# Channel attention and a gated MLP on one core: every engine's order from a planner, second bank seeded by a copy, five gate tiles

## The chip, the core and the metric

The kernel runs on 1 core of one Trainium2 chip. The metric is device time in microseconds: before, 2226.33 us, the median of three runs (2221.29 to 2227.1). TensorE (PE, with its weight loads as PEld), VectorE (DVE), ScalarE (ACT) and GpSimd (POOL) compute; SyncE (SP) issues the DMAs. Each engine works through its own list of instructions in order, and semaphores hold an instruction until its inputs are there.

## The reference

```python
B, N, C = (4, 6080, 256); d_ff = 2048
qn = q / (norm(q, axis=1) + 1e-06)          # q, k, v: (B, N, C) float32
kn = k / (norm(k, axis=1) + 1e-06)
s = kn.transpose(0, 2, 1) @ qn / tau        # C x C for each of 4 batches
a = exp(s - s.max(-1)); a /= a.sum(-1) + 1e-09
x = (v @ a).reshape(B * N, C)               # 24320 tokens
h = x @ w_in                                # w_in, w_out: float64
g = h * (1 / (1 + exp(-1.702 * h)))
out = (g @ w_out).astype(float32)
```

## The kernel before, in words

Every float32 product is made of rounded parts: a high part `h` (a cast by ACT, called `gh`, `vh`, `wh`, `qs`, `ks`) and the rest `l` (a subtraction on DVE, `gl`, `vl`, `wl`), and three matmuls, h by h, h by l, l by h.

Since `(v @ a) @ w_in = v @ (a @ w_in)`, each batch first gets its 256 x 256 matrix `a` from the scores (on PE, in the bank `s`, from q and k in 24 units of 2 x 128 tokens), its norms and a softmax, and then folded weights `a @ w_in`. These are combined with a Strassen scheme of seven products. The tokens of a batch go by in 6 chunks (five of 1024, one of 960), a chunk in two halves `n` of 512 (or 480) columns. For each chunk, 8 *pairs* of 128 hidden rows (`f` = 0, 1) are computed: 4 batches x 6 chunks x 8 pairs = 192 pairs.

A pair is seven products of three matmuls, into the PSUM banks `ps_x`, `ps_y`, `ps_z`. By the names of the new code, with the weight part and the part of `v` of each: m5 (z, 3, 3), m1 (x, 0, 0), m2 (y, 1, 1), m6 (x, 4, 4), m7 (x, 5, 5), m3 (z, 6, 2), m4 (x, 2, 6). The parts of `v` lie in tiles `px`, `py` (two buffers each) and `pz`, `pw` (one buffer), made from two loads, sums on POOL (line 500) and casts. Between the products ACT copies a bank to SBUF (`copied`, line 548: `r5` of z behind m5, `r1` of x behind m1, `r2` of x behind m6), and DVE adds (lines 562, 569, 571: `y + r1`, `x + r5` behind m7, `z + r2` behind m3). Out of these come four blocks, for each a gate (line 585, the activation, then its cast and low part) and a second projection `project` (line 604): six matmuls into one of two pairs of banks `ps_o`, summed over 16 hidden rows, then copied to `osb` (lines 614, 616) and stored.

Work beside it: in the first batch, w_in and w_out come as float64 words and are converted (`to_float32`, lines 131 to 145) during the first eight pairs, and each group of folded weights is made there. During each batch the next one's q and k are loaded, squared (ACT), added (POOL, line 267), split and multiplied, and its softmax and weights follow.

The order: pairs have four slots. `Hidden.slot` issues the products, and one `project` follows each slot, of the pair before in slots 0 to 2, and of block (0, 0) of the same pair in slot 3. Side work hangs on numbered slots. From the first pair on only PE keeps this order (`manual_schedule(engines={PE})`); the orders of DVE, ACT, POOL and SP come from a scheduler when the kernel is built, apart from what is `pinned` behind the newest copy.

Of the kernel before, what the change touches and what calls it, by code (L numbers as in the profile page):

```python
# [18 lines left out]
P = 128  # L19
# [8 lines left out]
def channel_attention_then_glu(  # L28
# [45 lines left out]
    gp = ctx.enter_context(tc.tile_pool(name="gp", bufs=2))  # L74
    op = ctx.enter_context(tc.tile_pool(name="op", bufs=2))
# [42 lines left out]
    def to_float32(out, raw, shape):  # L118

        lw = raw[..., 0]
        hw = raw[..., 1]
        z = cv.tile(shape, U32, tag="z", name="z")
        zf = z.bitcast(F32)
        eighths = cv.tile(shape, U32, tag="low", name="eighths")  # L130
        nc.scalar.activation(zf, hw.bitcast(F32), AF.Abs)
        nc.scalar.activation(eighths, lw, AF.Copy, scale=2.0**-29)
        yield
        nc.vector.tensor_scalar(zf, zf, F64_TOP, F64_BOTTOM, op0=ALU.min, op1=ALU.max)

        nc.vector.tensor_scalar(
            z, z, 5, 2, op0=ALU.logical_shift_left, op1=ALU.logical_shift_right
        )
# [6 lines left out]
        nc.vector.tensor_tensor(out.bitcast(U32), z, eighths, op=ALU.add)  # L145
        return out

    words = {}
# [14 lines left out]
    def win_convert(n):  # L163
        g, c = divmod(n, NC2)
        win[n] = sp.tile([P, GW], F32, tag=("raw_q", "raw_k")[c], name="win")
        yield from to_float32(win[n], words.pop(("in", n)), [P, GW])
# [7 lines left out]
    def wout_convert(u):  # L174
        t = yield from to_float32(None, words.pop(("out", u)), [P, 2, C])
        yield
        fs = slice(2 * u, 2 * u + 2)
        yield from split_parts(wo_h[:, fs, :], wo_l[:, fs, :], t)

    fetch = {"in": win_fetch, "out": wout_fetch}  # L180
    convert = {"in": win_convert, "out": wout_convert}


    class Attention:
        def __init__(self, b, direct=0):
# [5 lines left out]
            self.firsts = {}  # L191
# [54 lines left out]
        def prepare(self, u):  # L246
            nt = self.units[u][1]
            rq, rk = self.fetched(u)
            if u < self.direct:
                qs, ks = rq, rk  # L250
            else:

                qs = sp.tile([P, UT, 2, C], F32R, tag="qs", name="qs")
                ks = sp.tile([P, UT, 2, C], F32R, tag="ks", name="ks")
                for s, r in ((qs, rq), (ks, rk)):
                    split(s[:, :nt, 0, :], s[:, :nt, 1, :], r)
            for r, nm in ((rq, "acc_q"), (rk, "acc_k")):
                if u == 0:
                    acc = small.tile([P, UT, C], F32, tag=nm, name=nm)
                    setattr(self, nm, acc)  # L260
                    nc.scalar.activation(acc, r, AF.Square)
                else:
                    acc = getattr(self, nm)[:, :nt, :]
                    sq = sp.tile([P, UT, C], F32, tag="sq", name="sq", bufs=2)[:, :nt, :]
                    nc.scalar.activation(sq, r, AF.Square)  # L265
                    eng = nc.vector if self.alone else nc.gpsimd
                    eng.tensor_tensor(acc, acc, sq, op=ALU.add)  # L267
            return qs, ks
# [42 lines left out]
        def norms_a(self, meanwhile=None):  # L311

            assert UT == 2
            ps = bank("b", "ps_n")
            for n in range(2 * NC2):
                acc, i = (self.acc_q, self.acc_k)[n // NC2], n % NC2
                if i == 0:
                    eng = nc.vector if self.alone else nc.gpsimd
                    eng.tensor_tensor(acc[:, 0, :], acc[:, 0, :], acc[:, 1, :], op=ALU.add)
                nc.tensor.matmul(  # L320
                    ps[:, n : n + 1],
# [4 lines left out]
            if meanwhile is not None:  # L326
                meanwhile()
            self.rn = small.tile([P, 2 * NC2], F32, tag="rn", name="rn")
            nc.vector.tensor_copy(self.rn, ps[:, : 2 * NC2])
# [11 lines left out]
        def norms_c(self):  # L341

            ps = bank("c" if self.alone else "b", "ps_b")
            for i in range(NC2):
                nc.tensor.matmul(
                    ps[:, i * P : (i + 1) * P], lhsT=ones, rhs=self.diag[:, i, :],
                    start=True, stop=True,
                )
            self.rq = sp.tile([P, C], F32, tag="sq", name="rq", bufs=2)
            nc.vector.tensor_copy(self.rq, ps[:, :C])  # L350

        def softmax_a(self, meanwhile=None):
# [12 lines left out]
            if not self.alone:  # L365

                nc.vector.tensor_scalar_mul(m, m, -1.0)
            if meanwhile is not None:
                meanwhile()
            for i in range(NC2):  # L370
                x, z, mi = self.x[:, i, :], self.z[:, i : i + 1], m[:, i : i + 1]
                nc.scalar.activation(x, x, AF.Exp, bias=mi, accum_out=z)

            nc.scalar.activation(m, m, AF.Gelu_apprx_sigmoid)
# [9 lines left out]
        def transposes(self, meanwhile=None):  # L384
            self.aT_h = small.tile([P, NC2, C], F32R, tag="aT_h", name="aT_h")
            self.aT_l = small.tile([P, NC2, C], F32R, tag="aT_l", name="aT_l")
            ps = bank("b", "ps_t")
            psv = ps.rearrange("p (c x) -> p c x", c=NC2)
            for j in range(NC2):
                for i in range(NC2):  # L390
                    nc.tensor.transpose(  # L391
                        psv[:, j, i * P : (i + 1) * P],
# [3 lines left out]
            if meanwhile is not None:  # L396
                meanwhile()
            split(self.aT_h, self.aT_l, psv)
# [10 lines left out]
        def win_split(self, g, step=split):  # L409
            self.win_h, self.win_l = (  # L410
                sp.tile([P, NC2, GW], F32R, tag=t, name=n)
                for t, n in (("qs", "win_h"), ("ks", "win_l"))
            )
            done = [
                step(self.win_h[:, c, :], self.win_l[:, c, :], win.pop(NC2 * g + c))
                for c in range(NC2)
            ]
            if step is split:
                self.win_keep(g)
            return done  # L420
# [6 lines left out]
        def weights(self, g, i):  # L427
# [7 lines left out]
            ps = bank("ac"[i] if self.alone and g == 0 else "b", "ps_w")  # L435
            ci = slice(i * P, (i + 1) * P)
# [12 lines left out]
            src = ps.rearrange("p (q f n) -> p f q n", q=2, f=2)  # L449
            nc.scalar.copy(self.wf[0][:, (slice(0, 4, 3), slice(1, 3))[i]], src)  # L450

        def weight_sums(self, g):

            t, u = self.wf
            eng = nc.vector if self.alone and g == 0 else nc.gpsimd
            eng.tensor_tensor(u[:, 1], t[:, 0], t[:, 3], op=ALU.subtract)
            eng.tensor_tensor(t[:, 3], t[:, 3], t[:, 2], op=ALU.add)
            eng.tensor_tensor(u[:, 0], t[:, 3], t[:, 0], op=ALU.subtract)
            eng.tensor_tensor(u[:, 2], t[:, 1], u[:, 0], op=ALU.subtract)

        def weight_split(self, g, part, pair=None):

            if part == 0 and not pair:
# [3 lines left out]
            pairs = slice(0, 2) if pair is None else slice(pair, pair + 1)  # L467
            split(
# [408 lines left out]
```

## Time and profile before

| | |
|---|---|
| median of three runs | 2226.33 us |
| the profiled execution | 2224.45 us, span of its instructions 2222.7 us |
| PE, DVE, ACT, POOL busy | 2173.2, 1325.4, 1558.1, 432.0 us |
| granted TensorE clock, mean | 0.996 |
| matmuls recorded | 9952 |

Busy time is the time in which an instruction of the engine is under way. A matmul's end is modelled and lies behind the start of the next, so PE's busy time tells less than the distance between starts. The idle time of PE is given where no matmul is under way, with the engine and line that ended it.

### The profile page before, as it was taken

The page shows a single profiled execution, that of the slowest core. Times are in us where ns is not written, and L with a number is a line of the kernel's source. Part 1 is how long each engine was busy: PE and PEld are TensorE (multiplying, and loading weights), DVE is VectorE, ACT ScalarE, POOL GpSimd, SP SyncE. Part 2 cuts the span into 40 slices and gives each one's busy share as a digit, 9 for nine tenths or more (in the row PEclk, how much of TensorE's full clock was granted, in tenths as well). Part 3 has the DMA queues.
Part 4 walks back from the last instruction along what each step waited for, and adds up shares of the span by engine and source line. Part 5 has one row for each costly group of instructions (what it writes and reads, how often), then busy time and mean ns, then how long its engine had stood idle before and what let it go on. Part 6 is the DMA issues. An engine that isn't in the chain of part 4 may idle for free. (4 is left out here: it accounts for less than half of the span.)

```text
span 2222.7 us, 27468 instructions
## 1 busy us (share of the span) xinstructions
PE 2173.2 (98%) x9952; PEld 1807.5 (81%) x9952; DVE 1325.4 (60%) x1894; ACT 1558.1 (70%) x2769; POOL 432.0 (19%) x348
## 2 busy tenths in 40 slices
PE   8889999999999999999999999999999999999998
PEld 7668787888887888888888888788888888888887
DVE  7986646556555565665655656656555555555454
ACT  6777667767677776776767777677667666666665
POOL 1122313211121232231121213223112110010000
PEclk9999999999999999999999999999999999999999
DMA  9422213112111221221211212122012110111010
GB/s 350 149 85 69 76 48 95 55 66 65 50 64 48 76 86 58 76 60 60 66 57 56 89 47 84 58 76 73 29 56 76 37 57 20 39 57 30 27 37 18
DMA packets 72121, 151.47 MB, mean 68 GB/s; under 512 B 6704, under 2 KB 14128, under 8 KB 71984
## 3 DMA queue, kind: packets, MB, share of 16 engines
q1 hardware_dynamic: 71984, 149.71, 20.4%
q8 instruction: 78, 1.28, 0.2%
q14 instruction: 59, 0.48, 0.1%
HBM read 120.59 MB, written 29.10 MB: 67 GB/s over the span
## 5 line engine op out<-in xcount | busy, mean ns | idle before, releaser
L90 DVE TENSOR_TENSOR gl<-g,gh 128x512 fp32r<-128x512 f32 (+1 forms) x576 | 432.5, 757 | 334.9 <-ACT gh L89 334.7
L604 PE MATMUL ps_o<-gh,wo_l 128*128 128x512 f32 (+1 forms) x1536 | 596.9, 389 | 5.5 <-DVE wo_l L96 5.5
L604 PE MATMUL ps_o<-gh,wo_h 128*128 128x512 f32 (+1 forms) x1536 | 597.0, 389 | 1.5 <-ACT gh L89 1.0
L604 PE MATMUL ps_o<-gl,wo_h 128*128 128x512 f32 (+1 forms) x1536 | 472.6, 389 | 5.7 <-DVE gl L90 5.7
L89 ACT CAST gh<-g 128x512 fp32r<-128x512 f32 (+1 forms) x576 | 351.0, 618 | 9.9 <-PE ps_o L604 1.0
L604 PEld LDWEIGHTS ps_o<-gl,wo_h 128*128 128x128 f32 x1536 | 288.2, 188 | 67.1 <-DVE gl L90 9.8
L604 PEld LDWEIGHTS ps_o<-gh,wo_l 128*128 128x128 f32 x1536 | 289.0, 188 | 64.7 <-DVE wo_l L96 6.6
L604 PEld LDWEIGHTS ps_o<-gh,wo_h 128*128 128x128 f32 x1536 | 288.9, 188 | 61.5 <-ACT gh L89 2.0
L500 POOL TENSOR_TENSOR v_raw<-v_raw 128x512 f32<-128x512 f32 (+1 forms) x120 | 169.6, 1414 | 799.3 <-DMA v_raw<-in_vT 769.6
L540 PE MATMUL ps_x<-vh,wh 128*128 128x512 f32 (+1 forms) x768 | 302.5, 394 | 19.6 <-DVE r L569 11.7
L540 PE MATMUL ps_x<-vl,wh 128*128 128x512 f32 (+1 forms) x768 | 298.5, 389 | 0.0
L540 PE MATMUL ps_x<-vh,wl 128*128 128x512 f32 (+1 forms) x768 | 298.1, 388 | 0.0
L585 ACT ACTIVATE r<-r 128x512 f32<-128x512 f32 (+1 forms) x192 | 120.5, 627 | 235.5 <-DVE r L569 235.5
L548 ACT COPY r<-ps_x 128x512 f32<-128x512 f32 (+1 forms) x384 | 224.7, 585 | 35.6 <-PE ps_x L540 22.2
L562 DVE TENSOR_TENSOR ps_y<-ps_y,r 128x512 f32<-128x512 f32 (+1 forms) x192 | 133.0, 693 | 180.4 <-PE ps_y L540 175.0
L585 ACT ACTIVATE g<-ps_y 128x512 f32<-128x512 f32 (+1 forms) x192 | 114.0, 594 | 158.6 <-DVE ps_y L562 158.6
L90 DVE TENSOR_TENSOR gl<-r,gh 128x512 fp32r<-128x512 f32 (+1 forms) x192 | 140.0, 729 | 135.9 <-ACT gh L89 134.9
L267 POOL TENSOR_TENSOR acc_q<-acc_q,sq 128x512 f32<-128x512 f32 (+1 forms) x72 | 102.2, 1419 | 566.1 <-ACT sq L265 565.9
L569 DVE TENSOR_TENSOR r<-ps_x,r 128x512 f32<-128x512 f32 (+1 forms) x192 | 130.8, 681 | 117.7 <-PE ps_x L540 117.5
L540 PEld LDWEIGHTS ps_x<-vh,wh 128*128 128x128 f32 x768 | 144.6, 188 | 58.3 <-DVE r L569 17.5
L548 ACT COPY r<-ps_z 128x512 f32<-128x512 f32 (+1 forms) x192 | 112.4, 585 | 86.8 <-PE ps_z L540 86.4
L540 PEld LDWEIGHTS ps_x<-vh,wl 128*128 128x128 f32 x768 | 144.3, 188 | 29.6
(117 smaller groups left out, 3074.6 us busy)
## 6 DMA issues: line engine op xcount, KB each, us to landing
v_raw<-in_vT SPq DMA_DIRECT2D x80, 512.0 KB, 3.8
out_T<-osb SPq DMA_DIRECT2D x80, 256.0 KB, 2.1
raw_q<-in_q SPq DMA_DIRECT2D x69, 256.0 KB, 2.7
raw_k<-in_k SPq DMA_DIRECT2D x69, 256.0 KB, 2.8
win_h<-win_h SPq DMA_DIRECT2D x16, 512.0 KB, 4.1
win_l<-win_l SPq DMA_DIRECT2D x16, 512.0 KB, 3.2
v_raw<-in_vT SPq DMA_DIRECT2D x16, 480.0 KB, 3.6
raw_q<-in_q SPq DMA_DIRECT2D x6, 768.0 KB, 9.0
```

Source lines behind the costliest of these rows:

```text
L89: ins = nc.scalar.copy(dst_hi, src)
L90: nc.vector.tensor_tensor(dst_lo, src, dst_hi.bitcast(F32), op=ALU.subtract)
L267: eng.tensor_tensor(acc, acc, sq, op=ALU.add)
L500: nc.gpsimd.tensor_tensor(out, a, z, op=ALU.subtract)
L540: nc.tensor.matmul(out, lhsT=l[:, wi, :], rhs=r[:, n, : self.hw], start=first and m == 0, stop=last and m == 2, skip_group_check=True,)
L548: newest[0] = nc.scalar.copy(r, src)
L562: nc.vector.tensor_tensor(y, y, r1, op=ALU.add)
L569: nc.vector.tensor_tensor(self.r5, self.x, self.r5, op=ALU.add)
L585: nc.scalar.activation(g, src, AF.Gelu_apprx_sigmoid)
L604: nc.tensor.matmul(out[d][:, :w], lhsT=l[:, at_f, d * P : (d + 1) * P], rhs=r[:, :w], start=at_f == 0 and l is wo_h and r is gh, stop=at_f ...
```

## The change

All engines' orders are now written by a planner in the kernel. It books each instruction with a duration in units (a product of three matmuls is 1.0, ACT's and DVE's operations 0.75 to 1.9, the softmax's activations 5.8) and places it at the earliest time that its inputs and its engine allow; the instructions are then issued in the order of the planned times. For the first eight pairs (`together`) it takes, of those that are ready, the one with the longest path behind it. Side work lies in jobs that `advance` places in the gaps of ACT, DVE and POOL that the pair's own work leaves; score products go behind the first projection of a pair (block A), weight and norm products to two places behind m3 (block B).

Five things change in the pair itself. `r1` is gone: ACT copies `ps_x` into bank `ps_y` (the seed), and m2 adds to it. Where a norm, transpose or sum product has written only part of that bank, one matmul over its whole width is issued behind m1. The gate of block (0, 0) works in place in `ps_y`. There are five sets of gate tiles (three while the conversions use the other two), and from the tenth pair on all four second projections of a pair come in the next one, in the order (0, 0), (1, 1), (0, 1), (1, 0), the last two exchanged in a chunk's first pair. All output copies but the last are DVE's, with three buffers for them, and `r2` is DVE's in the pair of a softmax.

```diff
-    gp = ctx.enter_context(tc.tile_pool(name="gp", bufs=2))
-    op = ctx.enter_context(tc.tile_pool(name="op", bufs=2))
+    gp = ctx.enter_context(tc.tile_pool(name="gp", bufs=1))
+    op = ctx.enter_context(tc.tile_pool(name="op", bufs=3))
...
+    SETS = [(f"gh{n}", f"gl{n}") for n in range(5)]
+    ROOM = (4, 3)
...
-                y = bank("b", "ps_y")[:, :hw]
-                self.product(y, 1, 1, first=True, last=True)
-                nc.vector.tensor_tensor(y, y, r1, op=ALU.add)
-                self.gate(0, 0, y)
...
+    def m1(self):
+        self.x = bank("a", "ps_x")[:, : self.hw]
+        self.product(self.x, 0, 0, first=True)
+        y = bank("b", "ps_y")
+        if part_written[0]:
+            vh, _ = vparts[self.b, self.c, "px"]
+            full = vh[:, 0, :] if self.hw == NCH else wo_h[:, 0:2, :]
+            nc.tensor.matmul(y, lhsT=self.at.wh[self.fp // 2][:, 0, self.fp % 2, :], rhs=full, start=True, stop=True)
+            part_written[0] = False
+        self.y = y[:, : self.hw]
+    def m2(self):
+        self.product(self.y, 1, 1, last=True)
+    def seed(self):
+        nc.scalar.copy(self.y, self.x)
...
+    def gap(eng, dur, t):
+        for s, e in busy[eng]:
+            if t + dur <= s:
+                break
+            t = max(t, e)
+        return t
+    def base(eng, dur, t, token, deps, fn, *a):
...
+        t = gap(eng, dur, late(deps, t))
+        take(eng, dur, t)
+        emit(t, fn, *a)
+        done(token, t + dur)
...
+    def lay(p):
...
+        tensor(1.0, ("m5", p), [w[0], w[1], *v["py"], ("g", p - 1, 0, 1) if p else None], h.m5)
+        base("ACT", 1.0, 0, ("r5", p), [("m5", p), ("l", p - 1, 1, 1) if p else None], h.copied, "r5", "z", "ACT")
+        tensor(1.0, ("m1", p), [*v["px"], ("g", p - 1, 1, 0) if p else None, last_b[0]], h.m1)
+        base("ACT", 1.0, 0, ("seed", p), [("m1", p)], h.seed)
+        project(3)
...
+        if fp == 0:
+            for t in ("pw", "pz0", "pz1"):
+                for d in () if gather else v[t]:
+                    force(d)
+        block("A")
+        tensor(1.0, ("m6", p), [("seed", p)], h.m6)
...
+        tensor(1.0, ("m2", p), [], h.m2)
+        project(2)
+        gate(0, 0, "y", [("m2", p)])
...
+        tensor(1.0, ("m7", p), [("r2", p), *v["pz0"]], h.m7)
+        base("DVE", 1.05, 0, ("+5", p), [("m7", p), ("r5", p)], h.add, "r5", "x", "r5")
+        tensor(1.0, ("m3", p), [*v["pz1"]], h.m3)
...
+        project(1)
+        block("B")
+        tensor(1.0, ("m4", p), [("+5", p), *v["pw"]], h.m4)
...
+        project(0)
...
+    def turns(p):
+        swap = p % PAIRS == 0
+        second, third = ((1, 0), (0, 1)) if swap else ((0, 1), (1, 0))
+        old = [(p - 1, 1, 1), (p - 1, *second), (p - 1, *third)] if p else [None] * 3
+        if p < FIFTH:
+            return [*old, (p, 0, 0)]
+        if p == FIFTH:
+            return [*old, None]
+        return [(p - 1, 0, 0), *old]
```

PE, the middle of a pair without side work, before (`ps_x` is m1, then m6; `ps_y` is m2; `ps_o` a second projection):

```order
L540 MATMUL ps_x<-vh,wh 128x512
L540 MATMUL ps_x<-vl,wh 128x512
L540 MATMUL ps_x<-vh,wl 128x512
L540 MATMUL ps_y<-vh,wh 128x512
L540 MATMUL ps_y<-vl,wh 128x512
L540 MATMUL ps_y<-vh,wl 128x512
L604 MATMUL ps_o<-gh,wo_h 128x512
L604 MATMUL ps_o<-gh,wo_l 128x512
L604 MATMUL ps_o<-gh,wo_h 128x512
L604 MATMUL ps_o<-gh,wo_l 128x512
L604 MATMUL ps_o<-gl,wo_h 128x512 x2
L540 MATMUL ps_x<-vh,wh 128x512
```

PE, the same place now, in a pair with a score unit (`s`; most pairs of a chunk have one, the first has none); ahead of the first row stands m1's last matmul, behind the last one m6's remaining two and then m2:

```order
L590 MATMUL ps_x<-vh,wl 128x512
L670 MATMUL ps_o<-gh,wo_h 128x512
L670 MATMUL ps_o<-gh,wo_l 128x512
L670 MATMUL ps_o<-gh,wo_h 128x512
L670 MATMUL ps_o<-gh,wo_l 128x512
L670 MATMUL ps_o<-gl,wo_h 128x512 x2
L303 MATMUL s<-qs,ks 128x256 x12
L590 MATMUL ps_x<-vh,wh 128x512
```

m2 has moved from ahead of the projection to behind m6, so without a score unit six matmuls stand between m1 and m6 where nine stood.

DVE, ahead of the addition `r<-ps_x,r` behind m7, before (`qs`, `ks` are low parts of q and k, `gl` of a gate, `osb` an output copy):

```order
L90 TENSOR_TENSOR gl<-g,gh 128x512
L614 COPY osb<-ps_o 128x512
L90 TENSOR_TENSOR qs<-raw_q,qs 128x2x256
L90 TENSOR_TENSOR ks<-raw_k,ks 128x2x256
L569 TENSOR_TENSOR r<-ps_x,r 128x512
L571 TENSOR_TENSOR ps_z<-ps_z,r 128x512
```

DVE, in the same stretch of the program now:

```order
L659 TENSOR_TENSOR gl<-g,gh 128x512 x2
L276 TENSOR_TENSOR ks<-raw_k,ks 128x2x256
L659 TENSOR_TENSOR gl<-ps_y,gh 128x512
L639 TENSOR_TENSOR r<-ps_x,r 128x512
L639 TENSOR_TENSOR ps_z<-ps_z,r 128x512
L276 TENSOR_TENSOR qs<-raw_q,qs 128x2x256
L659 TENSOR_TENSOR gl<-r,gh 128x512
```

`qs` and `ks` no longer stand together, and the low part of the gate in `ps_y` stands directly ahead of the addition; it does so in 186 of 192 pairs.

ACT, around the softmax of the third batch, before (`x,z<-x,m` are the exponentials, between two table loads):

```order
L548 COPY r<-ps_z 128x512
L548 COPY r<-ps_x 128x512
L372 ACT_TABLE_LOAD
L372 ACTIVATE x,z<-x,m 128x256 x2
L585 ACT_TABLE_LOAD
L585 ACTIVATE g<-ps_y 128x512
L374 ACTIVATE m<-m 128x2
L89 CAST gh<-g 128x512
L548 COPY r<-ps_x 128x512
```

ACT, around the same softmax now; it comes in the first pair of the batch's last chunk (480 columns):

```order
L630 COPY r<-ps_z 128x480
L635 COPY ps_y<-ps_x 128x480
L405 ACT_TABLE_LOAD
L405 ACTIVATE x,z<-x,m 128x256 x2
L407 ACT_TABLE_LOAD
L407 ACTIVATE m<-m 128x2
L573 CAST vh<-v_raw 128x480 x3
L650 ACTIVATE ps_y<-ps_y 128x480
L655 CAST gh<-ps_y 128x480
```

The copy `r2` behind the block has gone to DVE, and three casts of `v` parts stand where the gate stood.

## Rows read from the trace of the kernel before

**Rows 1.** The page's first part: busy us (share of the span) xinstructions.
```profile
PE 2173.2 (98%) x9952; PEld 1807.5 (81%) x9952; DVE 1325.4 (60%) x1894; ACT 1558.1 (70%) x2769; POOL 432.0 (19%) x348
```

**Rows 2.** Timeline of an undisturbed pair: start us, us, engine, line, operation, tiles.
```profile
1900.53 0.40 PE L540 MATMUL ps_x<-vh,wl 128*128 128x512 f32 x1
...
1900.96 0.59 ACT L548 COPY r<-ps_x 128x512 f32<-128x512 f32 x1
...
1902.84 0.39 PE L540 MATMUL ps_x<-vh,wh 128*128 128x512 f32 x1
...
1904.88 0.39 PE L540 MATMUL ps_x<-vh,wh 128*128 128x512 f32 x1
```

**Rows 3.** Windows: stretch, length, busy us (x) of PE, PEld, DVE, ACT, POOL, clock.
```profile
65.70:175.30 109.60, 94.95 (x382) 72.47 (x382) 92.88 (x139) 86.18 (x154) 25.98 (x23) 0.97 0.32 106
175.30:2223.00 2047.70, 2018.87 (x9308) 1684.28 (x9306) 1181.92 (x1669) 1427.40 (x2544) 396.92 (x311) 1.00 0.18 58
60.00:100.00 40.00, 34.32 (x137) 26.02 (x136) 36.42 (x62) 31.84 (x58) 3.69 (x4) 0.96 0.35 119
277.60:281.00 3.40, 3.33 (x9) 2.66 (x10) 2.51 (x5) 3.08 (x6) 0.55 (x1) 0.62 0.70 233
```

**Rows 4.** PE's waits from 175.3 us: who waited for whom, us, times, longest.
```profile
PE ps_x L540 <- DVE r L569: 10.0, 9, 1.8
PE ps_x L540 <- ACT r L548: 7.1, 6, 2.1
PE ps_o L604 <- DVE gl L90: 4.9, 7, 0.8
PE ps_z L540 <- ACT g L585: 0.7, 3, 0.2
```

**Rows 5.** Timeline around the wait that ends at 277.68 us: DVE, POOL, PE.
```profile
274.15 1.18 DVE L90 TENSOR_TENSOR qs<-raw_q,qs 128x512 fp32r<-128x512 f32 x1
275.26 1.76 DVE L90 TENSOR_TENSOR ks<-raw_k,ks 128x512 fp32r<-128x512 f32 x1
276.94 0.68 DVE L569 TENSOR_TENSOR r<-ps_x,r 128x512 f32<-128x512 f32 x1
...
274.74 1.73 POOL L267 TENSOR_TENSOR acc_q<-acc_q,sq 128x512 f32<-128x512 f32 x1
...
277.68 0.50 PE L540 MATMUL ps_x<-vh,wh 128*128 128x512 f32 x1 [1.82 <-DVE r L569]
278.02 0.40 PE L540 MATMUL ps_x<-vl,wh 128*128 128x512 f32 x1
...
278.56 0.63 PE L604 MATMUL ps_o<-gh,wo_h 128*128 128x512 f32 x1
...
281.54 0.52 PE L540 MATMUL ps_z<-vl,wh 128*128 128x512 f32 x1
```

**Rows 6.** Timeline around a softmax: ACT and PE.
```profile
1079.37 1.28 ACT L372 ACT_TABLE_LOAD   x1
...
1083.07 0.60 ACT L585 ACTIVATE g<-ps_y 128x512 f32<-128x512 f32 x1
...
1084.86 0.50 PE L540 MATMUL ps_x<-vh,wh 128*128 128x512 f32 x1 [2.06 <-ACT r L548]
```

**Rows 7.** DVE's groups by form: xcount, busy us, mean ns, idle before and releasers.
```profile
L90 DVE TENSOR_TENSOR gl<-g,gh 128x512 fp32r<-128x512 f32 x480 | 366.8, 771 | 272.1 <-ACT gh L89 271.8
...
L562 DVE TENSOR_TENSOR ps_y<-ps_y,r 128x512 f32<-128x512 f32 x160 | 111.7, 698 | 152.1 <-PE ps_y L540 147.3 <-ACT qs L89 1.9 <-ACT r L548 1.7
```

**Rows 8.** The page's DMA issues, those of `v`: xcount, KB each, us to landing.
```profile
v_raw<-in_vT SPq DMA_DIRECT2D x80, 512.0 KB, 3.8
```

**Rows 9.** Timeline of the end: the last two output copies.
```profile
2218.23 0.66 DVE L614 COPY osb<-ps_o 128x480 f32<-128x480 f32 x1 [2.17 <-DMA out_T<-osb]
2218.88 0.56 ACT L616 COPY osb<-ps_o 128x480 f32<-128x480 f32 x1 [2.69 <-DMA out_T<-osb]
```

More of the change, by code (lines that the diff above doesn't have):

```diff
@@ new lines, in start_up, with emit @@
+        at.weights_copy(1)
+        for n in range(4):
+            at.weight_sum(0, n)
+        for part in range(2):
+            for low in (False, True):
+                at.weight_split(0, part, 0, low)
+        v_part(0, 0, "pz", None, True)
+        next(s1)
+        next(s1, None)
+    LAG = 0.15
+    gather = []
+    events = []
+    ends = {}
+    busy = {e: [] for e in ("ACT", "DVE", "POOL")}
+    jobs = []
+    maker = {}
+    blocks = {"A": [], "B": []}
+    now = [0.0]
+    def emit(t, fn, *a):
+        events.append((t, len(events), fn, a))
@@ new lines, in channel_attention_then_glu, with force, advance, block @@
+    floor = [0.0]
+    def force(token):
+        if token is None or token in ends:
+            return
+        job = maker[token]
+        while token not in ends:
+            for d in job.ops[0][3]:
+                force(d)
+            assert job.step(None)
+    def advance(pair, limit):
+        for job in sorted(jobs, key=lambda j: j.due):
+            while job.begin <= pair and job.ops and job.step(limit):
+                pass
+        jobs[:] = [j for j in jobs if j.ops]
+    def block(where):
+        for job in blocks[where]:
+            if late(job.ops[0][3], 0.0) <= now[0] + 0.5:
+                job.run()
+                return
@@ new lines, in channel_attention_then_glu, with room_at, finish @@
+    free = [(0.0, n, None) for n in range(3)]
+    def room_at(t, token):
+        free.sort()
+        end, n, last = free.pop(0)
+        waiting[token] = n
+        return n, last
+    waiting = {}
+    opened_sets = []
+    last_b = [None]
+    def finish(q, f, n):
+        hq = pairs[q]
+        key = (hq.b, hq.c, n)
+        begins = key not in opened
+        opened[key] = opened.get(key, 0) + 1
+        closes = opened[key] == NF
+        deps = [("l", q, f, n), ("cv", "out", hq.fp, 7)]
+        if begins:
+            deps += [("left", n, d) for d in range(NC2) if ("left", n, d) in ends]
+        tensor(2.0, ("j", q, f, n), deps, hq.project, f, n, begins, closes)
+        room = waiting.pop(("g", q, f, n))
+        free.append((len(opened_sets) if gather else now[0], room, ("j", q, f, n)))
+        opened_sets.append(room)
+        if closes:
+            for d in range(NC2):
+                e = "ACT" if d and q == TOTAL - 1 else "DVE"
+                base(e, 1.05, 0, ("left", n, d), [("j", q, f, n)], hq.leave, n, d, e)
@@ new lines, in channel_attention_then_glu @@
+    with tc.manual_schedule():
+        start_up()
+        busy["DVE"].append((-9.0, 2.0))
+        together(PAIRS)
+        for p in range(PAIRS, TOTAL):
+            if p == PAIRS:
+                free += [(now[0], n, ("cv", "out", 7 - (n == 3), 7)) for n in (3, 4)]
+            lay(p)
+            t = now[0]
+            advance(p, {"ACT": t + 1.0, "DVE": t + 9.0, "POOL": t + 12.0, "SP": t + 9.0})
+        for f, n in ((0, 0), (1, 1), (0, 1), (1, 0)):
+            finish(TOTAL - 1, f, n)
+        assert not jobs
+        for _, _, fn, a in sorted(events, key=lambda e: e[:2]):
+            fn(*a)
```

1013 lines of the change are left out of this document (698 added, 315 removed).

## The prediction

> **What bounds the kernel now.** I read the page's first part, then windows by stage, then TensorE's waits, then the timeline around single waits. PE is busy 98% [rows 1], but a matmul's modelled end lies past the start of the next, so the share hides how the time is made. In an undisturbed pair nine matmuls start in 2.04 us, 0.227 us each, while a row shows 0.39 us [rows 2]: 0.16 us of drain is counted as busy. A pair has 45 matmuls, 10.2 us; with 192 pairs nearly all of the span is matmuls at that spacing, which the change leaves alone. What can go is the time in which PE does not issue.
>
> There are two places for it. In the first eight pairs (65.7 to 175.3 us), where the weights are converted beside the gates, 382 matmuls take 109.6 us [rows 3]; at 0.227 us they would take 86.7, so 22.9 us are lost. DVE is busy 92.88 us of these 109.6, so it is nearly as long as PE's floor. After 175.3 us PE waits 22.7 us, in 25 waits [rows 4]. Each costs more than its row: 0.16 us of hidden drain, and 0.34 us instead of 0.227 until the second matmul [rows 5], together 0.27; 25 of them make 6.8. Behind the wait that ends at 277.68 us the granted clock of the stretch is 0.62 [rows 3], and seven matmuls start in 2.98 us instead of 1.59 [rows 5], which is the lower level (1.2 of 2.4 GHz): 1.4 us more. So 30.9 us can be had there, 22.9 before it.
>
> The waits are of two kinds. At 277.68 us PE waits for the DVE addition `r<-ps_x,r`. It had nothing to wait for itself; it stood behind `qs` and `ks`, which took 1.18 and 1.76 us beside a POOL addition [rows 5], where a low part alone takes 0.77 or less [rows 7]. At 1084.86 us PE waits 2.06 us for ScalarE's copy, behind the softmax: from the first table load to the next gate 3.70 us [rows 6].
>
> **The change part by part.** *The order in the first eight pairs* goes to a list of ready operations, longest remaining path first. It removes no conversion; DVE loses the eight additions `ps_y<-ps_y,r`, 0.69 us each [rows 7], 5.5 us. DVE's work there becomes 92.88 - 5.5 = 87.4 us, PE's floor 86.7: two engines with the same work, each waiting for the other at times. The densest 40 us of this part have DVE busy 36.42 [rows 3], 91%. I take that share throughout: 87.4 / 0.91 = 96.0 us, a gain of 13.6. The ends: no gain where DVE's order is as bad as before, 22.2 where DVE never idles. The cover for the conversions' ScalarE halves is ScalarE itself, 86.18 us busy of 109.6; it loses no work, so under 96 us it is 90% full. That is why I don't go below 96.
>
> *The order behind it.* Before, only PE's order was laid down; DVE's came from the scheduler, which put `ks`, a `v` part, a weight part or an output copy directly ahead of the addition that m4 (the product of part 6 into `ps_x`) waits for. In the new order `gl<-ps_y,gh` stands there in 186 of 192 pairs. It has one SBUF input where `ks` has two. The score parts are split up and end at least a pair before their matmuls, so I see no new wait there. A late low part of a gate, 7 waits and 4.9 us before [rows 4], now meets a later projection: that of block (0, 0) stands in the next pair, behind its m1, and that of (0, 1), once the first in the next pair, is the third. I let 3 us of all these stay.
>
> The softmax stays as long. Its block stands behind the seed copy, and `r2` moves to DVE for that pair. But three casts of `v` (`pw` and both halves of `pz`) stand behind the block, and m7, which comes behind m6 and m2, reads the first half of `pz`. Counted from m1's last start plus drain: seed 0.59, block 3.83 (3.70 and 0.13 for the small activation that now lies inside it), two casts some 1.0, DVE's low part 0.65, with hand-overs 6.3 us; PE is there after 4.08 (projection 1.36, m6 and m2 0.68 each, projection 1.36). So 2.2 us and 0.27 are lost, 2.5 in each of three batches, 7.5 us, about what it was. Left are 10.5 of 30.9; the gain is 20.4 us. The ends: 30.9, and 2.8 (the first rival).
>
> *The seed.* m1's `ps_x` is copied by ScalarE into bank `y` and m2 accumulates on it, so 192 copies to SBUF become 192 copies to PSUM. No row shows that form; the nearest are the copy to SBUF, 0.59 us [rows 2], and an addition that writes PSUM in place, 0.70 on DVE [rows 7]. I take 0.59; at 0.70 nothing changes as long as it hides. Its cover: m6 waits for it, and between them stands one projection, 6 x 0.227 = 1.36 us. In [rows 2] m1's last matmul starts at 1900.53 and the copy at 1900.96, so it ends 1.02 us after; m6 can start after 1.36 + 0.23 = 1.59. The slack is 0.5 us, where it was 1.2 with three more matmuls between. DVE loses 192 additions and gains 46 output copies and 3 `r2`, off PE's path. The gate on `ps_y` in place takes no SBUF tile and holds bank `y` longer; only weight products, norms and the next seed use that bank, behind its low part.
>
> Where bank `y` was written in part, one matmul marks all its columns: 10 more matmuls in the new order, 10 x 0.227 = +2.3 us, on the path.
>
> *Loads and stores.* SP's and POOL's instructions are the same in number; only their places change. A `v` load is booked with 6.0 units of 0.68 us, 4.1; the page has 3.8 us to landing for each of its two transfers [rows 8], the second issued behind the first, so POOL's sums and the cast behind them can come about 1 us late, and the cast holds up ScalarE. Behind it stands work with about 1 us of slack. 23 loads make 0 to 23 us; I take 1, inside the 3 above. With three output buffers instead of two, the last copy waits for the first of the last stores and not the second: 2218.88 - 2218.23 [rows 9], -0.6 us. `leave` on DVE alone comes at chunk ends, ahead of a lot of idle.
>
> *Sum,* against the profiled execution: 2224.45 - 13.6 - 20.4 + 2.3 - 0.6 = 2192.2 us, 1.5% under the median of 2226.33; that execution lies 0.1% under the median, within the spread of the three runs (2221.29 to 2227.1). I forecast 2192.
>
> **The rivals.** *The waits for held DVE operations stay.* In [rows 5] `ks` takes 1.76 us because POOL adds beside it, and `gl<-g,gh` averages 0.77 over 480 [rows 7], so this happens all along, and the planner books 1.15 units (0.78 us) whatever POOL does. If as many such waits remain, 16 with 10.0 + 4.9 us [rows 4] and 0.27 each, 19.2, with the softmax 7.5 and the slow clock 1.4, then 28.1 of 30.9 stay and the time is 2209.8. Against it: what stands ahead of the addition. The Trainium skill (SBUF — State Buffer, section SBUF: two separate sides) says that a VectorE operation with two SBUF inputs and a GpSimd operation share a port pair held for a whole instruction, the other blocking fully. The rows at 274 to 277 us agree (1.18 and 1.76 us beside a POOL addition), and by that rule this rival holds for any place where a two-input low part still precedes such an addition.
>
> *Slower: the seed's slack is too small.* The copy `r5` stands directly ahead of the seed and waits for DVE's low part of the previous pair. If it ends 0.62 us late (one ScalarE operation), m6 waits 0.12 and 0.27, 0.39 in each of the 184 pairs behind the first eight: 72 us, 2264. It decides from the point where 32.3 us are eaten: waits in two pairs of three (32.3 / 0.27 = 120). Against it: before, the same one projection stood between m6 and m7, with ScalarE's `r2` between, and `ACT r` shows 6 waits in all [rows 4], not 184; and the last pairs of the kernel ran at 0.227 us throughout. The Trainium skill (TensorE: Matmul & The Clock Gate, Part 1) says that ScalarE and VectorE take their instructions strictly in order; the block at 1079 us agrees (the copy behind it is late by as much), and by that rule a planned place that is wrong costs all that stands behind it.
>
> *The order moves waits but not their sum.* If the 30.9 us come back elsewhere and the first eight pairs give only the 5.5 of the removed additions: 2224.45 - 5.5 + 2.3 - 0.6 = 2220.7. For it: the waits stand where side work falls, and all of that work remains. Against it: both engines have idle time to spread it over (DVE 60%, ACT 70% busy [rows 1]).
>
> **How the numbers follow.** Forecast (2178 to 2205) 0.62; better, down to 2173 with both gains whole, 0.05; held DVE operations (2205 to 2218) 0.17; waits moved 0.07; slower 0.09. A measurement tells 0.3%, some 7 us, from no change: faster 0.84, same 0.07, slower 0.09. The range is 2175 to 2217.
>
> **What would show it.** Right: the first eight pairs take 92 to 100 us; PE's waits behind them sum to 6 to 12 us, the largest of them three of 2 us, for `vl` in m7 or `ACT r`, in the pair of the softmax; hardly a wait for `DVE r`; m6 waits for `ps_y` nowhere; matmuls that fill a bank, 10. Wrong: many short waits of `ps_x` for the seed; first pairs over 104 us; waits for DVE's `r` of 8 us or more; a spacing other than 0.227 us.

## The result, and the profile after

The changed kernel takes 2205.19 us (median of four runs, 2203.73 to 2206.24) against 2225.32 us of the kernel before beside it: a ratio of 0.9912, 95% interval 0.9894 to 0.9929, 20 us faster. Forecast were 2192 us. The profiled execution took 2205.02 us, with a span of 2203.2 us. The page's first part answers to [rows 1]:

```profile
PE 2170.1 (98%) x9962; PEld 1817.1 (82%) x9962; DVE 1215.9 (55%) x1780; ACT 1551.7 (70%) x2749; POOL 409.7 (19%) x348
```

PE has 10 more matmuls, the forecast number. The windows of [rows 3], cut where pairs 0 and 8 start now (stretch, length, busy us and count of PE, PEld, DVE, ACT, POOL, clock), with two stretches of pair 6:

```profile
66.60:178.80 112.20, 96.52 (x381) 74.89 (x380) 88.20 (x136) 86.19 (x157) 27.05 (x23) 0.91 0.31 104
178.80:2203.20 2024.40, 2012.97 (x9316) 1690.34 (x9314) 1076.64 (x1557) 1420.57 (x2518) 373.51 (x312) 1.00 0.18 59
151.00:156.00 5.00, 1.44 (x3) 0.72 (x4) 5.00 (x4) 2.57 (x6) 5.00 (x4) 0.50 0.00 0
156.00:160.00 4.00, 4.00 (x10) 3.14 (x11) 1.88 (x2) 2.24 (x4) 3.04 (x3) 0.50 0.00 0
```

The stretch behind the first eight pairs fell from 2047.4 us (2222.7 - 175.3) to 2024.4, by 23.0 where 18.7 were forecast (20.4 - 2.3 + 0.6). The first eight pairs did not fall by 13.6 us but rose by 2.6, from 109.6 to 112.2, and they start 0.9 us later. So the miss lies in this stretch, 5% of the span. PE's waits behind it answer to [rows 4] (who waited for whom, us, times, longest):

```profile
PE ps_x L590 <- ACT vh L573: 4.5, 3, 1.5
PE ps_x L590 <- ACT g L650: 0.9, 1, 0.9
PE ps_x L590 <- DVE vl L571: 0.8, 3, 0.3
PE ps_x L590 <- ACT ps_y L635: 0.2, 1, 0.2
```

22.7 us in 25 waits became 6.4 us in 8. The waits for DVE's `r` and `gl` are gone, and the seed (`ACT ps_y`) holds m6 once in 184 pairs (in the first eight, twice, 0.8 us in all). What is left is the softmax, three times; it answers to [rows 6] (ACT, DVE and PE of that pair):

```profile
541.46 1.28 ACT L407 ACT_TABLE_LOAD   x1
...
542.87 1.56 ACT L573 CAST vh<-v_raw 128x480 fp32r<-128x480 f32 x3
...
543.99 0.49 PE L590 MATMUL ps_x<-vh,wh 128*128 128x480 f32 x1 [1.51 <-ACT vh L573]
...
544.75 0.49 PE L590 MATMUL ps_x<-vl,wh 128*128 128x480 f32 x1 [0.28 <-DVE vl L571]
```

m7 waits for the cast of `pz` behind the exponentials, as worked out: 1.51 + 0.28 us here. In the first eight pairs PE's waits sum to 15.6 us, 14.4 before, at other places; the four largest now:

```profile
PE ps_z L590 <- ACT wh L518: 7.3, 3, 2.9
PE ps_z L590 <- DVE wl L516: 3.7, 2, 3.4
PE ps_x L590 <- DVE r L639: 1.9, 1, 1.9
PE ps_o L670 <- DVE gl L659: 1.6, 1, 1.6
```

`ps_z` is m5, the first product of a pair. It stands at 96.41, 123.10 and 151.13 us, in the first pair of weight groups 1, 2 and 3 (a group is the folded weights of two pairs), and waits for that group's parts, the casts `wh` and the low parts `wl`. DVE's work did shrink, from 92.88 to 88.20 us, but DVE is busy 79% of the stretch, not 91%.

### The profile page after: what moved, and what is told of

It reads as the page before. It is cut to its first block, busy times and chain, and to the rows that moved or that the text cites. A ratio compares the mean times of both kernels' runs of the same rounds, so it can differ in the third digit from the quotient of the medians.

```text
span 2203.2 us, 26843 instructions
## 1 busy us (share of the span) xinstructions
PE 2170.1 (98%) x9962; PEld 1817.1 (82%) x9962; DVE 1215.9 (55%) x1780; ACT 1551.7 (70%) x2749; POOL 409.7 (19%) x348
## 4 chain that ended last, share of the span: by engine, by line
PE 94%; DVE 2%; ACT 2%; DMA 1%; issue 1%; SPq 0%; POOL 0%; DVEq 0%; ACTq 0%; POOLq 0%
PE ps_o L670 46%; PE ps_x L590 23%; PE ps_z L590 12%; PE ps_y L590 6%; PE s L303 5%; PE ps_w L485 2%; DVE acc_k L296 0%; ACT sq L289 0%; DMA raw_k<-in_k 0%; DMA words<-in_w_in 0%; DVE vl L571 0%; POOL v_raw L554 0%; DMA v_raw<-in_vT 0%; ACT vh L573 0%; SPq L244 0%
## 5 line engine op out<-in xcount | busy, mean ns | idle before, releaser
L659 DVE TENSOR_TENSOR gl<-ps_y,gh 128x512 fp32r<-128x512 f32 (+1 forms) x192 | 131.8, 686 | 503.9 <-ACT gh L655 503.9
L659 DVE TENSOR_TENSOR gl<-g,gh 128x512 fp32r<-128x512 f32 (+1 forms) x384 | 283.2, 777 | 164.0 <-ACT gh L655 163.9
L630 ACT COPY r<-ps_x 128x512 f32<-128x512 f32 (+1 forms) x189 | 110.3, 584 | 219.0 <-PE ps_x L590 218.1
L655 ACT CAST gh<-g 128x512 fp32r<-128x512 f32 (+1 forms) x384 | 216.0, 612 | 0.1
L296 POOL TENSOR_TENSOR acc_q<-acc_q,sq 128x512 f32<-128x512 f32 (+1 forms) x72 | 91.4, 1269 | 635.3 <-ACT sq L289 614.1
L659 DVE TENSOR_TENSOR gl<-r,gh 128x512 fp32r<-128x512 f32 (+1 forms) x192 | 144.7, 754 | 70.7 <-ACT gh L655 67.7
L590 PEld LDWEIGHTS ps_x<-vl,wh 128*128 128x128 f32 x768 | 145.0, 189 | 27.4 <-DVE vl L571 1.7
L630 ACT COPY r<-ps_z 128x512 f32<-128x512 f32 (+1 forms) x192 | 112.2, 584 | 74.9 <-PE ps_z L590 73.8
L590 PE MATMUL ps_z<-vh,wh 128*128 128x512 f32 (+1 forms) x384 | 150.1, 391 | 7.3 <-ACT wh L518 7.3
```

Of the source, the lines that this page charges most:

```text
L296: eng.tensor_tensor(acc, acc, self.sq.pop((u, n)), op=ALU.add)
L590: nc.tensor.matmul(out, lhsT=l[:, wi, :], rhs=r[:, n, : self.hw], start=first and m == 0, stop=last and m == 2, skip_group_check=True,)
L630: nc.scalar.copy(r, getattr(self, src))
L655: nc.scalar.copy(gh, g)
L659: nc.vector.tensor_tensor(gl, g, gh.bitcast(F32), op=ALU.subtract)
```

## Experiments

All edits are to the changed kernel; "first eight" is the window from the first product of pair 0 to that of pair 8 in the profiled execution. Where nothing of that stretch was edited (`soft`, `same_pair`) it took 112.7 and 113.0 us, so less than 1 us there tells nothing. One wait for a gate (`ACT g`, 0.4 to 2.5 us) stands in most of these kernels at the edge of the window, just behind it, in `sq_dve` inside it.

**The first eight pairs: booked durations (`measured`), VectorE's work (`light`), the place of the split (`split_early`).**

```diff
-            self.eng, self.dur, self.token, ... = eng, dur, token, ...
+            dur *= {"ACT": 0.78, "DVE": 0.78, "POOL": 1.15}.get(eng, 1.0); self.eng, ...
```

> The changed kernel, and one line of its planner: in the list for the first eight pairs, ScalarE's and VectorE's operations are booked with 0.78 of the old number of units and GpSimd's with 1.15. A cast is booked with 1.0 unit (0.68 us), but back to back casts start 0.52 us apart in the trace after; a low part is booked with 1.15 units (0.78 us) and they start 0.61 us apart; a GpSimd sum is booked with 0.88 us and takes 1.0. Nothing is computed in another way. In the trace after, the first eight pairs take 112.2 us. Theory B (booking: the list believes ScalarE and VectorE full, and so lays the conversion of the next weight group behind work that is not urgent): first eight pairs 99 to 106 us, the waits for wh and wl at the first product of a weight group halved, 2192 to 2199 us in all. Theory C (chain: each weight group needs two products in one bank, one per pair, four GpSimd sums and eight splits, whatever is booked): 109 to 112 us, 2202 to 2205. Theory W (VectorE has too much work there): 108 to 112 us, as VectorE's work does not change.

```diff
+        few = out is None
...
+        full = z; z, zf, hw, eighths = (x[:, :1, :32] if few else x for x in (z, zf, hw, eighths)); ...
```

> The changed kernel, with the four VectorE steps in the conversion of w_out done on 32 of 512 columns only, so the output is not the reference's; every engine's order stays as it was. In the trace after, these steps take 0.42, 0.43, 0.69 and 0.69 us, eight times, 17.8 us; on 32 columns I put them at 0.1 each, 3.2, so VectorE's 88.2 us in the first eight pairs become 73.6. Theory W (VectorE's work sets the time): the pairs shrink with it, at the same share busy (0.79) to 93.6 us of 112.2, and the whole to about 2187. Theories B and C (the order, or the chain of the weight group, sets it): the waits for wh and wl at the first product of a group stay, since w_in's conversion and the weight sums are untouched; 107 to 112 us, 2200 to 2205.

```diff
-            deps = [(*key, "+", 3)]
+            deps = [(*key, "+", 3 if b else 1)]
...
-                deps = [(*key, "s", p, o, 0)]
+                deps = [(*key, "s", p, o, 0), *([] if b or not g else [(*key, "+", 3)] if (p, o) == (0, 1) else [])]
```

> The changed kernel; in the first batch the planner may book the first split of a weight group (the casts wh and low parts wl of its first four parts) behind the second of the four GpSimd sums instead of the fourth. The data allow it: only the first two sums write these parts. In the trace after, the last three sums of the groups start at 92.83, 118.31 and 147.66 us and take 0.83 to 1.0 each, so the second sum is there at 93.8, 119.3 and 148.5; the casts stand at 95.75, 122.43 and 150.45, 1.9, 3.1 and 1.9 us later, and the first product of the group waits for them (2.3 to 3.0 us more than the usual step). Theory C (the chain of the weight group, as planned, sets the time): these waits shrink by 1.9 to 3.1 us each, 5 to 7 us in all, the low clock behind them too; first eight pairs 105 to 107 us, 2198 to 2200. Theory A (ScalarE and VectorE are so full that something else is late by as much): first eight pairs 110 to 112.5, 2203 to 2206.

Measured: 2201.47 (ratio to before 0.9898, 0.9877 to 0.9918), 2202.48 (0.9904, 0.9887 to 0.9921) and 2201.46 us (0.9893, 0.9878 to 0.9907). Each interval overlaps that of the changed kernel (0.9894 to 0.9929), so I go by the windows, one row of each kernel, in this order:

```profile
66.70:176.60 109.90, 96.85 (x381) 74.35 (x380) 85.78 (x136) 87.10 (x157) 25.43 (x23) 0.94 0.32 106
```
```profile
67.00:174.90 107.90, 92.79 (x382) 72.62 (x381) 75.97 (x136) 85.61 (x157) 24.77 (x22) 0.95 0.33 108
```
```profile
66.80:174.30 107.50, 95.00 (x382) 73.76 (x381) 87.51 (x136) 85.86 (x157) 26.47 (x23) 0.95 0.32 108
```

Theory W falls: 12.2 us less VectorE work (88.20 to 75.97) gave 4.3 us; in proportion it would have given 15.6. With all that idle time PE still waited at the same places, m5 for `wh` and `wl`, nearly as long as before (10.2 us for 11.0):

```profile
PE ps_z L590 <- ACT wh L518: 6.2, 3, 2.9
PE ps_z L590 <- DVE wl L516: 4.0, 2, 3.8
```

The booking alone gave 2.3 us, less than theory B wanted. The earlier split alone gave 4.7, a little less than theory C's least (5.2); its waits of m5 for `wh` fell from 7.3 to 3.9 us:

```profile
PE ps_z L590 <- ACT wh L518: 3.9, 3, 1.8
PE ps_z L590 <- DVE wl L516: 2.4, 2, 2.0
```

**GpSimd beside VectorE (`sq_dve`).**

```diff
-                eng = nc.vector if self.alone else nc.gpsimd
+                eng = nc.vector if self.alone or u < self.direct else nc.gpsimd
```

> The changed kernel; the six additions of squares of the next batch's first four units, which GpSimd does from 150 to 164 us, are VectorE's. TensorE's order stays. In the trace after, three low parts wl take 3.89 us there (0.68, 0.68 and 0.55 where GpSimd is idle, 1.9 in all) and the third matmul of the group's first product waits 3.83 us for one of them. Theory P (a GpSimd addition beside it holds a VectorE operation with two SBUF inputs): the low parts take 2.0 to 2.6 us, that wait falls by 2 us or more, the low clock behind it (0.50 from 151 to 160 us) gives another 1 to 2 back; first eight pairs 107 to 110 us, 2200 to 2203. Theory Q (the low part is late because of what stands ahead of it; VectorE gets 6 x 0.69 = 4.1 us more work): 112 to 115 us, 2205 to 2208.

Measured: 2205.48 us (0.9905, 0.9887 to 0.9923), first eight 113.7. The timeline of the changed kernel, then of this one, POOL, DVE and m5:

```profile
151.79 1.72 POOL L554 TENSOR_TENSOR v_raw<-v_raw 128x512 f32<-128x512 f32 x1
152.31 1.75 DVE L181 TENSOR_TENSOR wo_l<-z,wo_h 128x512 fp32r<-128x512 f32 x1
153.48 1.71 POOL L296 TENSOR_TENSOR acc_k<-acc_k,sq 128x512 f32<-128x512 f32 x1
153.99 3.89 DVE L516 TENSOR_TENSOR wl<-wf,wh 128x512 fp32r<-128x512 f32 x3
155.15 1.72 POOL L296 TENSOR_TENSOR acc_q<-acc_q,sq 128x512 f32<-128x512 f32 x1
155.79 0.80 PE L590 MATMUL ps_z<-vh,wl 128*128 128x512 f32 x1 [3.43 <-DVE wl L516]
```
```profile
150.34 3.39 POOL L554 TENSOR_TENSOR v_raw<-v_raw 128x512 f32<-128x512 f32 x2
...
152.53 1.74 DVE L296 TENSOR_TENSOR acc_q<-acc_q,sq 128x512 f32<-128x512 f32 x1
154.20 1.15 DVE L516 TENSOR_TENSOR wl<-wf,wh 128x512 fp32r<-128x512 f32 x2
154.93 0.80 PE L590 MATMUL ps_z<-vh,wl 128*128 128x512 f32 x1 [2.36 <-DVE wl L516]
```

The price of contention is shown: one by one the three low parts `wl` of the first row take 1.74, 1.62 and 0.68 us, the first two beside a GpSimd addition, the third behind it; in the second timeline, without GpSimd, the first two take 0.68 and 0.54 (the second of them has 384 columns). It is not what sets the time. m5's third matmul needs the first of them only, so the wait fell by what that one lost, 1.1 us. Ahead of it stands a held operation in both kernels (`wo_l`, 1.75 us, before; now an added one, 1.74 beside the `v` sums). And the stretch is no shorter: a wait for a gate, 1.8 us, now ends at pair 8's first product; in the changed kernel one of 0.9 us comes behind it.

**The softmax (`soft`).**

```diff
+        if fp == 0 and any(j.ops and j.ops[0][2] == ("soft", b + 1, "exp") for j in jobs):
+            for t in ("pw", "pz0", "pz1"):
+                for d in v[t]:
+                    force(d)
         tensor(1.0, ("m5", p), [w[0], w[1], *v["py"], ...
```

> The changed kernel; in the pair of a softmax the three casts of v parts (pw and the two of pz) are booked before the pair, ahead of the block of exponentials instead of behind it. In the trace after, m7 waits for these casts three times, 1.67 us beyond the usual step and 0.55 for the low part behind it. Theory M (the casts alone hold m7): these waits go, 3 x 2.2 = 6.7 us, and the pairs take 11.7 us instead of 13.9: 2198 to 2199. Theory N (ScalarE has 3.8 us more than it can hold in that pair, so the gates behind the block make the next product wait): 0 to 3 us gained, waits for g or gh in the same pair or the next; 2202 to 2205.

Measured: 2196.72 us (0.9874, 0.9860 to 0.9889), theory M; 1.8 us of the 8.5 gained are more than the 6.7 that it put on the three waits. Behind the first eight pairs (from 178.2 us) these two waits of PE remain, none at a softmax; the first ends at 181.5 us and was 0.9 in the changed kernel:

```profile
PE ps_x L590 <- ACT g L650: 2.5, 1, 2.5
PE ps_x L590 <- ACT ps_y L635: 0.2, 1, 0.2
```

**What earned the 23 us behind the first eight pairs: the seed, the later projection, or the orders.**

```diff
+            self.r1 = gp.tile([P, NCH], F32, tag="r1", name="r")[:, : self.hw]
-            nc.scalar.copy(self.y, self.x)
+            nc.scalar.copy(self.r1, self.x)
...
+        base("DVE", 1.05, 0, ("+1", p), [("m2", p), ("seed", p)], h.add, "y", "y", "r1")
```

> The changed kernel without the seed: ScalarE copies ps_x to an SBUF tile as before the change, m2 starts bank y itself, and VectorE adds the copy into ps_y (192 additions of 0.69 us); no matmul is needed to fill the bank; two output buffers instead of three make room for the tile. If the additions are hidden beside PE behind the first eight pairs (VectorE is busy 53% there): 10 fills less, -2.3 us, 5.5 us more VectorE work in the first eight pairs, worth 0 to 7 us, last store +0.6; 2203 to 2211. If the additions were a part of what made PE wait (they stand ahead of the gate, in front of the addition that m4 waits for): waits for r or gl in many pairs, 5 us or more of them, 2212 to 2225.

```diff
-    FIFTH = PAIRS + 1
+    FIFTH = B * NCHUNK * PAIRS
```

> The changed kernel with the second projection of block (0, 0) in its own pair throughout, as in its first nine pairs, instead of one turn later; five gate sets stay. Theory T (the later turn is what took the waits for low parts of gates away; before the change there were 7 of them, 4.9 us): waits of ps_o for gl come back, 3 to 10 us with restarts, 2208 to 2215. Theory U (gl of (0, 0) has four turns of other work in front of its projection anyway, about 4.8 us from m2 to the projection against 2.5 us for gate, cast and low part): no wait comes back, 2203 to 2207.

```diff
     with tc.manual_schedule():
         start_up()
+    with tc.manual_schedule(engines={mybir.EngineType.PE}):
```

> The changed kernel, of whose plan only TensorE's order is kept behind the start; VectorE's, ScalarE's, GpSimd's and SyncE's instructions are ordered by the scheduler at build time, as before the change. Theory O (the planned order of VectorE and ScalarE is what removed the waits behind the first eight pairs): waits of PE for r, gl and copies are back, 15 to 25 us of them behind the first eight pairs, and with 0.27 us each for the restart the time is 2222 to 2240. Theory S (the structure removed them: projections a pair later, the seed, five gate sets give every operation more room): fewer than 5 us of waits beside the softmaxes, 2203 to 2212.

> The changed kernel; TensorE, ScalarE, GpSimd and SyncE keep the planned order, VectorE's instructions behind the start are ordered by the scheduler at build time. With only TensorE's order kept the kernel took 2275.83 us, 70 more than the changed one, and the run doesn't tell which engine's order does it. Theory D (VectorE's order: before the change 9 waits, 10.0 us, were for the addition r and 7, 4.9 us, for gl): such waits are back, 6 to 15 us and 0.27 each, 2212 to 2225. Theory A (ScalarE's order: in that run 31 us of the waits behind the first eight pairs name ScalarE and 8 VectorE): 2204 to 2211.

> The same with ScalarE's instructions alone ordered by the scheduler, VectorE's by the plan. Theory A: most of the 70 us, 2240 to 2275, with waits of PE for gates (g), copies (r, ps_y) at the chunks' first pairs. Theory D: 2205 to 2215.

Measured, with the window behind the first eight pairs (2024.4 us in the changed kernel):

| kernel | us | ratio to before | first eight | behind |
|---|---|---|---|---|
| `no_seed` | 2217.77 | 0.9971 (0.9956 to 0.9985) | 113.2 | 2032.9 |
| `same_pair` | 2205.88 | 0.9916 (0.9901 to 0.9930) | 113.0 | 2024.8 |
| `pe_only` | 2275.83 | 1.0233 (1.0216 to 1.0250) | 113.8 | 2086.7 |
| `dve_sched` | 2214.28 | 0.9958 (0.9944 to 0.9971) | 115.9 | 2028.0 |
| `act_sched` | 2256.02 | 1.0149 (1.0135 to 1.0163) | 108.5 | 2073.0 |

The later projection of block (0, 0) earns nothing that shows (theory U). Without the seed 8.5 us come back behind the first eight pairs: 12 waits for `r` of 6.7 us and 0.27 each make 9.9, 9 fills less take 2.0, a later last store adds 0.8. The other waits grew as well, from 6.4 us to 8.0, so these terms add up to more than was measured. The 8.5 is from the profiled execution, the fastest of seven (2214.57 us); the median is 12.6 us above the changed kernel's. The row of the waits, and one of the twelve (VectorE, ScalarE and m4):

```profile
PE ps_x L590 <- DVE r L636: 6.7, 12, 0.7
```
```profile
378.19 0.69 DVE L636 TENSOR_TENSOR ps_y<-ps_y,r 128x512 f32<-128x512 f32 x1
...
378.92 0.58 ACT L647 ACTIVATE ps_y<-ps_y 128x512 f32<-128x512 f32 x1 [1.74 <-DVE ps_y L636]
380.15 0.69 DVE L656 TENSOR_TENSOR gl<-ps_y,gh 128x512 fp32r<-128x512 f32 x1 [0.68 <-ACT gh L652]
380.76 0.68 DVE L636 TENSOR_TENSOR r<-ps_x,r 128x512 f32<-128x512 f32 x1
...
381.49 0.50 PE L590 MATMUL ps_x<-vh,wh 128*128 128x512 f32 x1 [0.70 <-DVE r L636]
```

The gate waits for the addition into `ps_y`, its low part is late by that, and `r` stands behind the low part. The seed took the addition out of this row.

Of the orders it is ScalarE's that counts (theory A): with the scheduler's order of it the stretch behind takes 48.6 us more, with VectorE's 3.6. As a whole `dve_sched` lies in theory D's range, but the profiled execution's 9.6 us more are 2.3 ahead of pair 0, 3.7 in the first eight pairs and 3.6 behind, and behind them PE waits for `r` once, 0.8 us, and never for `gl`. Waits of PE in `act_sched`, the three largest, and one place:

```profile
PE ps_x L590 <- DVE r L639: 13.5, 15, 1.8
PE ps_x L590 <- ACT g L650: 11.0, 12, 1.8
PE ps_x L590 <- ACT ps_y L635: 8.4, 14, 1.5
```
```profile
296.16 0.63 ACT L289 ACTIVATE sq<-raw_q 128x512 f32<-128x512 f32 x1 [0.77 <-DMA raw_q<-in_q]
297.83 0.63 ACT L289 ACTIVATE sq<-raw_k 128x512 f32<-128x512 f32 x1 [1.04 <-DMA raw_k<-in_k]
298.37 0.61 ACT L650 ACTIVATE r<-r 128x512 f32<-128x512 f32 x1
...
301.34 0.59 ACT L650 ACTIVATE g<-ps_x 128x512 f32<-128x512 f32 x1
...
301.99 0.50 PE L590 MATMUL ps_x<-vh,wh 128*128 128x512 f32 x1 [1.03 <-ACT g L650]
```

The squares stand ahead of the gates and wait for a load, and m1 pays. The 15 waits that name DVE's `r` come in a kernel whose VectorE keeps the plan. Ahead of each, DVE itself stood idle, 3.8 to 5.2 us, until ScalarE's cast `gh` came; one of them:

```profile
310.79 0.69 DVE L659 TENSOR_TENSOR gl<-ps_y,gh 128x512 fp32r<-128x512 f32 x1 [4.69 <-ACT gh L655]
...
312.14 0.50 PE L590 MATMUL ps_x<-vh,wh 128*128 128x512 f32 x1 [0.91 <-DVE r L639]
```

The kernel before had helps (`pinned`) that `act_sched` and `pe_only` lack, so these 48.6 us are not what the plan gained over it. In the first eight pairs the scheduler's order of ScalarE does better than the plan (108.5 us, though they start 4.5 us later).

**All together (`all_parts`), and the same with GpSimd's work left on GpSimd (`pool_sums`).** Beside the parts above (the softmax's is written a little differently), the first weight sum is booked behind the first copy:

```diff
-                deps = [(*key, "+", n - 1)] if n else [(*key, "c", 1)]
+                deps = [(*key, "+", n - 1), *([(*key, "c", 1)] if n == 1 else [])] if n else [(*key, "c", 0)]
```

> The changed kernel with the pieces that the other runs point to: the softmax pair's casts ahead of the exponentials (2196.72 alone), first splits behind the second sum (first eight pairs 112.2 to 107.4 alone), the booked durations at 0.78 (to 109.9 alone); new: in the first batch the first sum is booked behind the first of the two copies, all four sums and the six additions of squares are VectorE's instead of GpSimd's. If the gains add up: 2205.2 - 8.5 - 4.8 - 2.3, and the three sums on VectorE (128x256, 0.4 us instead of 1.0 each) take 1 to 2 us from each of three groups' chains, 2184 to 2189, first eight pairs 99 to 103 us. If VectorE, which gets 12 x 0.4 + 6 x 0.69 = 9 us more work on 88 in the first eight pairs, is the next bound: they stay at 105 to 109, 2190 to 2196.

> The kernel all_parts with the four sums of each weight group and the six additions of squares back on GpSimd; the booking, the earlier split and the softmax pair as in all_parts. In all_parts the first eight pairs took 99.0 us, 13.2 less than in the changed kernel; the earlier split alone gave 4.8 and the booking alone 2.3, so 6.1 are not told apart. Theory G (GpSimd is a part of the weight group's chain: a sum of 1.0 us there against 0.4 on VectorE, and its long additions hold VectorE's): first eight pairs 103 to 106 us, 2186 to 2190. Theory J (the earlier split and the booking are worth more together than apart): 99 to 101 us, 2182 to 2185.

Measured: 2182.17 (0.9812, 0.9798 to 0.9825) and 2185.79 us (0.9831, 0.9813 to 0.9849). First eight, and for `all_parts` the stretch behind, in which PE has no wait:

```profile
66.80:165.80 99.00, 92.03 (x381) 70.99 (x380) 89.02 (x155) 86.37 (x159) 7.19 (x5) 0.98 0.36 117
165.80:2180.10 2014.30, 2009.04 (x9316) 1688.09 (x9315) 1071.66 (x1557) 1418.77 (x2517) 369.78 (x311) 1.00 0.18 59
```
```profile
66.50:165.80 99.30, 92.23 (x381) 71.31 (x380) 87.16 (x136) 86.68 (x158) 23.18 (x20) 0.98 0.35 114
```

Theory J: who does the sums makes no difference to the first eight pairs (99.0 and 99.3 us). Three edits to the planner's numbers, with no operation removed or moved to another engine, take 12.9 us out of them; alone two of them gave 2.3 and 4.7. The third was not run alone. The whole of `pool_sums` is 3.6 us longer, 2.4 of it behind the first eight pairs, where GpSimd's `v` sums come at 167.4 us (160.1 in `all_parts`) and a product waits 1.5 us for a cast behind them. `all_parts` beats both kernels, the one before by 40 us (2222.49 beside it).

## Why the prediction was right, and where it was wrong

The time lies inside the stated range, in part by luck: of the 16.2 us missed in the first eight pairs and the 0.9 ahead of them, 4.3 were made up by a gain larger than forecast behind them. 2205.19 us also stands on the border between the forecast's band (to 2205) and that of the held DVE operations (2205 to 2218), so the time alone doesn't tell the two apart; the waits do.

**The first eight pairs, forecast 96.0 us, measured 112.2: this step failed.** It divided VectorE's remaining work, 87.4 us (88.20 measured), by the share of the densest 40 us, 0.91, and took that share for granted "throughout". The work was right, the share was 0.79. The step treated the stretch as a throughput of VectorE. It is a chain for each weight group: two products in one bank, sums, splits, and m5 at its end. The planner stretched that chain by booking the first split behind a sum it does not need and by booking ScalarE's and VectorE's operations 28% too long (1 / 0.78). `light` shows that work was not the limit, `pool_sums` that the plan was: with 87.16 us of work in 99.3 the share is 0.88, close to the 0.91 I had assumed. The 3.3 us from 96.0 to 99.3 stay open. I had read the list's rule, longest remaining path first, without checking the paths that it was given.

The long waits cost a second time. From 151 to 160 us, behind m5's wait of 2.88 us and through the next of 3.43, the granted clock is 0.50, the lower level; over the first eight pairs it is 0.91, against 0.97 before [rows 3] and 0.98 in `all_parts`.

**The waits behind, 10.5 us left of 30.9: right.** 6.4 us in 8 waits, with 0.27 each 8.6; that is a gain of 22.3 for 20.4. The softmax is the largest and sits where it was put, 5.3 us in six waits, 6.9 with 0.27 each, for the 7.5 forecast with restarts. Less 9 fills (one of the 10 lies in the first eight pairs) at 0.227 us, with the time behind the last matmul 0.8 us shorter (5.8 to 5.0) for 0.6, this makes 21.1 of the 23.0 measured; 1.9 us I can't place.

**The reason given for it was half right.** I put it on what stands ahead of DVE's addition. The rows before agree: each of the nine waits for `r` stood directly behind `qs` and `ks`, with `ks` at 1.76 to 1.78 us; that pair stood there in 46 of 184 pairs, and now in none. But no run brings it back: `dve_sched` has it there 3 times, in 57 other pairs a single score or weight part, and one wait. So what took these nine waits away is not shown, nor what took the seven for `gl`. The seed, in the planned order, keeps twelve other waits for `r` away and is worth 8.5 us; to this side effect on VectorE's row I gave no price outside the first eight pairs ("off PE's path"). And the queue that must be right is ScalarE's, which the prediction weighed only at the softmax and in a rival. At the softmax the prediction says that the copy behind the block of 3.70 us is late "by as much"; it starts 2.8 us behind the end of m6.

**The seed: right.** The copy to PSUM takes 0.57 us for the 0.59 taken, and m6 comes as worked out (m1's last matmul, the copy, m6):

```profile
1850.55 0.39 PE L590 MATMUL ps_x<-vh,wl 128*128 128x512 f32 x1
1850.98 0.57 ACT L635 COPY ps_y<-ps_x 128x512 f32<-128x512 f32 x1
...
1852.14 0.39 PE L590 MATMUL ps_x<-vh,wh 128*128 128x512 f32 x1
```

The copy ends at 1851.55, 0.59 us ahead of m6; 0.5 was forecast.

**The rivals.** Held VectorE operations do not make PE wait behind the first eight pairs (no wait for `r` or `gl`), but they do in pair 6 (`wl`, 3.43 us). The slower case, m6 held in most pairs, did not come: 0.2 us once. That waits only move was true of the first eight pairs: VectorE lost 4.7 us of work, and PE's waits are 15.6 us for 14.4.

## What to carry to other kernels

Where a stretch has several nearly full engines, don't forecast it by work over an assumed share: follow the chain that each late wait ends, and look whether every dependency and duration booked in it is a real one. A planned order is only as good as its numbers, and they cost nothing to mend. An operation taken off an engine with much idle time can still pay, if it stood in a short chain (addition, gate, low part, addition) that a product waits for.

## What the runs showed of the hardware

A VectorE low part beside a GpSimd addition took 1.62 to 1.75 us, about as long as the addition beside it (1.71 or 1.72), against 0.54 to 0.69 alone; moving six of the eight additions away was still worth nothing. ScalarE's copy from one PSUM bank to another took 0.57 us, to SBUF 0.59. From 151 to 160 us PE stood at the lower clock level (granted 0.50), with waits of 2.88 us ahead and 3.43 us inside; behind the second the matmuls from 156.38 to 160.22 us still start 0.43 us apart, in a row.
